# Two edits to the last layer of an attention + gated-MLP kernel: eight pairs at another place modulo 512 bytes, and a group of loaded values in each of two places

## Chip, cores and metric

One core of one Trainium2 chip. The metric is device time in microseconds (us) of one execution, the median of the runs shown. Engines are named as the profile names them: PE is the matrix engine (PEld its weight loads), DVE, ACT and POOL work on vectors, SP issues most of the DMA transfers.

## What is computed

Linear attention with exponential features, and then a gated two-layer MLP on its output, all in float32. Cut to what matters:

```python
# q, k, v: (8, 8, 576, 64); omega: (128, 64)
q_p, k_p = phi(q * scale), phi(k * scale)     # exp(x omega^T - |x|^2/2 - max) / sqrt(m)
num = einsum('bhsm,bhmd->bhsd', q_p, einsum('bhsm,bhsd->bhmd', k_p, v))
den = einsum('bhsm,bhm->bhs', q_p, sum(k_p, axis=2))[..., None] + 1e-06
x = (num / den) as (4608 tokens, 512)
gate = 1 / (1 + exp(-(x @ w_gate)))           # w_gate, w_val: (512, 1536)
out = (gate * (x @ w_val)) @ w_out            # w_out: (1536, 512)
```

## The kernel before

A float32 product is made of three matmuls in the type fp32r: each operand is split into a high part (`yh`, `wh`) and what is left (`yl`, `wl`), and `yl*wh + yh*wl + yh*wh` is summed. The MLP's large products are also cut by a scheme with seven block products instead of eight (`PRODUCT`; the seven operands have index 0 to 6, `N_OPS = 7`).

The program has three stretches. First the attention, which a planner orders with modelled times (`Turns`), mixed with a first part of the MLP (L531: all tokens against the first four of the twelve 128-wide column tiles). Then `second_pass` (L631) makes the other columns, token chunk by token chunk, 128x384 matmuls. The results of both go to DRAM: `ye` holds the values of the first `EP = 2` pairs of column tiles, `yl` (the DRAM tensor) those of the other four pairs, with all seven combinations. Last comes `last(g)` for g = 0 to 17, the last layer: it multiplies the gated values with `w_out`. The change is here.

A group `g` is two times 128 tokens. For each group the loop runs over `j`, the `NPAIR = 6` pairs; below, (g, j) names a pair of a group. For a pair:

- `gated_values` loads its values into a tile `yr` (SP issues it). For j below 2 that is three transfers from `ye`, and `sums` (L741, DVE, four instructions) makes the other combinations. For j of 2 and more it is one transfer of 448 KB from `yl` (L736).
- `parts_of` splits them: ACT copies the values rounded into `yh` (L749), then DVE, or POOL for j = 5 and g above 0, subtracts to get the rest, `yl` (L751). `yh` and `yl` each take one of eight buffers (`buffer`), so four pairs are held at a time, and a buffer comes free when PE has done the pair that lay in it.
- PE does 21 matmuls (L800), 128x128 by 128x256: for each of the seven products the three of the split. The values are the operand that is loaded into the array, the weights `u` are the operand that streams.

After the six pairs, ACT and DVE combine seven sums into the output (`p1`, L816, and seven `add`, L613), and ACT's queue stores it.

The place of a loaded tile before: for g = 0, pairs 0 and 1 lie in the two buffers of tag `xr`, and pairs 2 to 5 in one buffer of tag `u` (as large as one pair of column weights). From g = 1 on, even pairs take turns in the two buffers of `xr`, odd pairs in the two buffers of `ya`, so four pairs are loaded or in use at a time. During group 0 the first three pairs of group 1 are asked for ahead (L808); after that the loads stand in the program at their pair, and the compiler's scheduler sets the engines' order.

The place of `yh` and `yl`: in their buffer, `APART = 16` floats, 64 bytes, from the front. With that the values of a matmul lie 64 bytes behind its streaming weights modulo 512 bytes, in all 2268 matmuls of the last layer. In `second_pass` and in the L531 products both operands of a matmul lie at the same place modulo 512 bytes, which this document calls level.

Of the kernel before, what the change touches and what calls it, by code (L numbers as in the profile page):

```python
# [9 lines left out]
F32 = mybir.dt.float32  # L10
# [10 lines left out]
P = 128  # L21
# [22 lines left out]
NPAIR = NJ // 2  # L44
NE = 4
EP = NE // 2
# [8 lines left out]
UL, UE = 5, 3  # L55


BELOW, APART = 80, 16

FILL = 1e6  # L60
# [26 lines left out]
N_OPS = 7  # L87
# [142 lines left out]
def attn_glu_kernel(ctx: ExitStack, tc, qT, kT, qn, kn, va, om, ident, w, out):  # L230
# [30 lines left out]
    def any_bank(name):  # L261

        n_banks[0] += 1
        return bank(n_banks[0] % 8, name)
# [5 lines left out]
    def pin(ins):  # L270
        return tc.keep_in_program_order(ins) if pinned else ins
# [4 lines left out]
    class Ring(Shelf):  # L276
# [6 lines left out]
        def next(self):  # L283
            return next((p for p in self.places if p[1] == self.at), None)
# [147 lines left out]
    def buffer(name):  # L432
        at, n = (late, XL) if turn_of[0] % (XL + XE) < XL else (tail, XE)
        turn_of[0] += 1
        return at.tile([P, 2, 2, W], F32R, tag="x", bufs=n, name=name)
# [52 lines left out]
    def chunk_loads():  # L488
        for i, (o, n) in enumerate(chunks):
            t = yield from after(arrived[i], 0)  # L490
            t, (r,) = yield from turn("SP", t, xrring)
            raw = load(o, n)
            t = dma(t, 2 * n, KC)
            last = Event(turns, KC)
            for k in range(KC):
                t, (place,) = yield from turn("ACT", t, xring)
                x = keep.tile([P, 2, NC], F32R, tag="x", bufs=XK, name=f"xe{o}_{k}")[:, :, :n]
                nc.scalar.activation(out=x[:, 0], in_=raw[:, k], func=AF.Copy)  # L498
                th = use("ACT", t, act(n), LAG)
                x_of[i, k] = x, place  # L500
                turns.start(chunk_low(i, k, x, raw, n, th, last), -1)
            t = yield from after(last, t)
            xrring.put(r, t)

    def chunk_low(i, k, x, raw, n, t, last):
        t = yield "POOL", t, None, None
        nc.gpsimd.tensor_tensor(out=x[:, 1], in0=raw[:, k], in1=x[:, 0].bitcast(F32), op=ALU.subtract)  # L507
        t = use("POOL", t, pool_(n), LAG)
        x_ready[i][k].set(t)
        last.set(t)  # L510
# [101 lines left out]
    def add(o, a, b):  # L612
        return nc.vector.tensor_tensor(out=o, in0=a, in1=b, op=ALU.add)  # L613
# [70 lines left out]
    def put():  # L684
        while stores:
            to, y = stores.pop(0)
            pin(nc.sync.dma_start(out=to, in_=y))
# [35 lines left out]
        assert not plan  # L723
        return held

    def gated_values(g, j, raw=None):

        if raw is None:
            raw = tail.tile([P, 8, P], F32, tag=("xr", "ya")[j % 2], bufs=2, name=f"yr{g}_{j}")
        t = g // SUB * NW + g % SUB * P  # L730
        if j < EP:
            one, two, both = ye[j, :, 1, t + W : t + W + P], ye[j, :, 0, t + W : t + W + P], ye[j, :, :, t : t + P]
            for to, x in ((raw[:, :2], both), (raw[:, 2], one), (raw[:, 7], two)):
                pin(nc.sync.dma_start(out=to, in_=x))
        else:
            pin(nc.sync.dma_start(out=raw[:, :N_OPS], in_=yl[j - EP, :, g]))  # L736
        return raw

    def sums(raw, pin=lambda x: x):
        for o, a, b, op in ((4, 7, 2, ALU.add), (3, 4, 0, ALU.subtract), (5, 0, 7, ALU.subtract), (6, 1, 3, ALU.subtract)):  # L740
            pin(nc.vector.tensor_tensor(out=raw[:, o], in0=raw[:, a], in1=raw[:, b], op=op))  # L741

    def parts_of(g, j, raw, pin=lambda x: x):
        yh, yl_ = (
            buffer(f"{t}{g}_{j}").rearrange("p a b t -> p (a b t)")[:, APART : APART + N_OPS * P].rearrange("p (o t) -> p o t", t=P)
            for t in ("yh", "yl")
        )
        x = raw[:, :N_OPS]
        pin(nc.scalar.activation(out=yh, in_=x, func=AF.Copy))  # L749
        engine = nc.gpsimd if j == NPAIR - 1 and g else nc.vector  # L750
        pin(engine.tensor_tensor(out=yl_, in0=x, in1=yh.bitcast(F32), op=ALU.subtract))  # L751
        return yh, yl_

    first, ahead = {}, []

    def first_values():

        raws = [gated_values(0, j, tail.tile([P, 8, P], F32, tag="xr", bufs=2, name=f"yr0_{j}")) for j in range(2)]

        def parts(j):  # L760
            first[j] = parts_of(0, j, raws[j], pin)

        def others():
            both = tail.tile([P, NPAIR - 2, N_OPS, P], F32, tag="u", bufs=UE, name="yr0_2")
            raws.extend(gated_values(0, j, both[:, j - 2]) for j in range(2, NPAIR))
            first["raws"] = raws

        c = NCW - 1
        return {
            (c, 2, 2): [lambda: sums(raws[0], pin)],  # L770
            (c, 3, 2): [lambda: sums(raws[1], pin)],
            (c, 7, 0): [lambda: parts(0)],
            (c, 7, 1): [others],
            (c, 7, 2): [lambda: parts(1)],
        }

    def last(g, held=None):

        po = [any_bank(f"po{i}_{g}") for i in range(4)]

        at = {
            n: po[i][:, h * Q : (h + 1) * Q]
            for i, ns in enumerate(((1,), (6, 7), (5, 2), (3, 4))) for h, n in enumerate(ns)
        }
        pin_ = pin if g == 0 else lambda x: x
        for j in range(NPAIR):
            if g == 0 and j in first:
                yh, yl_ = first[j]
            else:
                raw = first["raws"][j] if g == 0 else ahead.pop(0) if ahead else gated_values(g, j)  # L790
                if j < EP:
                    sums(raw)
                yh, yl_ = parts_of(g, j, raw, pin_)
            wh, wl = units[2 * (NPAIR - EP) + j]
            for n, o in at.items():
                i, k = PRODUCT[n]
                i = PLACE[i]
                for m, (u, v) in enumerate(((yl_, wh), (yh, wl), (yh, wh))):
                    pin_(
                        nc.tensor.matmul(  # L800
                            o, lhsT=u[:, i, :], rhs=v[:, k, :],
                            start=(j + m == 0 and n in (1, 6, 5, 3)), stop=(j == NPAIR - 1 and m == 2),
                            skip_group_check=True,
                        )
                    )
            if j == 0 and held is not None:
                next(held, None)
                ahead[:] = [gated_values(1, i) for i in range(3)]  # L808
            elif j == 1 and held is not None:
                put()  # L810
        p1, u2, u3 = (
            late.tile([P, Q], F32, tag=t, bufs=n, name=f"{t}o{g}") for t, n in (("p1", 2), ("u2", 2), ("u3", 1))
        )
        os = tail.tile([P, 2, 2, Q], F32, tag="yb", bufs=1, name=f"o{g}")
        o1, o2 = os[:, 0], os[:, 1]
        nc.scalar.activation(out=p1, in_=at[1], func=AF.Copy)  # L816
        add(u2, at[6], p1)
        add(u3, at[7], u2)
        add(u2, at[5], u2)
        add(o2[:, 1], at[5], u3)  # L820
        add(o1[:, 0], at[2], p1)
        add(o1[:, 1], at[3], u2)
        add(o2[:, 0], at[4], u3)
        t = g // SUB * NW + g % SUB * P
        if g < NCW * SUB - 1:
            for o, r in ((o1, t), (o2, t + W)):
                nc.scalar.dma_start(out=out[r : r + P, :], in_=o)
            return
        for engine, o, i, r in ((nc.sync, o2, 1, t + W), (nc.scalar, o1, 0, t), (nc.scalar, o1, 1, t), (nc.sync, o2, 0, t + W)):
            engine.dma_start(out=out[r : r + P, i * Q : (i + 1) * Q], in_=o[:, i])  # L830
# [298 lines left out]
    with tc.tile_pool(name="early", bufs=1) as early, tc.tile_pool(name="keep", bufs=1) as keep:  # L1129
        with tc.manual_schedule():  # L1130
            with (
# [4 lines left out]
                for key, rank in sorted(order.items(), key=lambda x: x[1]):  # L1136
                    n, *a = key
                    if n[0] == "n":
                        u, b = a
# [53 lines left out]
    tail = ctx.enter_context(tc.tile_pool(name="tail", bufs=1))  # L1193
# [75 lines left out]
```

## Time and profile before

| what | value |
|---|---|
| median of 3 runs | 1081.38 us (1076.92, 1081.38, 1082.26) |
| profiled execution, its own time | 1091.19 us |
| its span, first to last instruction | 1089.4 us |
| PE busy | 1057.5 us, 97% |
| DVE, ACT, POOL busy | 773.0, 490.7, 407.2 us |
| last layer, first to last matmul | about 811.9 to 1084.8 us of the span |

All times of day below are microseconds from the start of the profiled span. The profiled execution is 9.8 us longer than the median of the runs; differences between places of the trace are taken inside the trace. A matmul's shown length (some 280 ns here) is longer than its step to the next one, since matmuls overlap; the pace is read from the starts.

### The profile page before, as it was taken

The numbers are of one execution on the slowest core, as the hardware profiler recorded it, in microseconds if no ns is written. First come the engines' busy times: TensorE is split into PE (matmuls) and PEld (weight loads), VectorE is DVE, ScalarE is ACT, GpSimd is POOL, SyncE is SP. The second block draws the span as 40 slices with busy tenths as digits, with TensorE's granted clock in tenths as the row PEclk, the third lists the DMA queues.
The fourth block names the chain that finished last, engine by engine and source line by source line (L and its number), as shares of the span: only waits on it lengthen the run. The fifth ranks groups of instructions, "written<-read, shape, count | busy, mean of one in ns | idle before, by whom it ended". The sixth has DMA issues, their size and how long they took to land.

```text
span 1089.4 us, 26466 instructions
## 1 busy us (share of the span) xinstructions
PE 1057.5 (97%) x10556; PEld 982.9 (90%) x10556; DVE 773.0 (71%) x1482; ACT 490.7 (45%) x1026; POOL 407.2 (37%) x326
## 2 busy tenths in 40 slices
PE   6789999999999999999999999999999999999998
PEld 5778887878878878899999999999999899999998
DVE  3889998998888856457747574756657777666664
ACT  5777756776456445333323232323223444443442
POOL 0342433342343332126756676756553111111111
PEclk9889999999999999999999999999999999999999
DMA  7587979998768648152424324142897566666663
GB/s 280 179 265 258 323 249 352 306 347 281 264 203 305 226 152 323 48 204 81 146 102 141 121 95 166 52 159 102 295 377 234 185 209 201 191 197 191 197 197 104
DMA packets 121323, 226.32 MB, mean 208 GB/s; under 512 B 10992, under 2 KB 59888, under 8 KB 118128
## 3 DMA queue, kind: packets, MB, share of 16 engines
q1 hardware_dynamic: 115872, 215.39, 58.6%
q10 hardware_dynamic: 5328, 9.24, 2.3%
q8 instruction: 83, 1.36, 0.5%
q14 instruction: 40, 0.33, 0.1%
HBM read 144.90 MB, written 79.69 MB: 206 GB/s over the span
## 4 chain that ended last, share of the span: by engine, by line
PE 87%; DVE 5%; DMA 3%; issue 2%; ACT 2%; POOL 1%; SPq 0%; DVEq 0%; POOLq 0%; ACTq 0%
PE gw L631 32%; PE po L800 23%; PE gv L531 15%; PE pkv L1004 4%; PE ppk L922 3%; PE ppq L922 3%; PE pnq L1069 3%; PE ptq L1052 3%; PE pxq L1094 1%; DMA yr<-yl 1%; ACT kpk L980 1%; DMA xT<-xsq 1%; POOL xe L507 1%; DVE xq L1086 1%; DVE yl L751 1%
## 5 line engine op out<-in xcount | busy, mean ns | idle before, releaser
L631 PE MATMUL gw<-xl,u 128*128 128x384 f32 x2016 | 350.5, 334 | 0.0
L631 PEld LDWEIGHTS gw<-xl,u 128*128 128x128 f32 x2016 | 349.3, 188 | 0.9 <-issue 0.9
L800 PE MATMUL po<-u,yh 128*128 128x256 f32 x1512 | 266.8, 281 | 0.0
L800 PEld LDWEIGHTS po<-u,yh 128*128 128x128 f32 x1512 | 232.9, 190 | 0.0
L800 PE MATMUL po<-u,yl 128*128 128x256 f32 x756 | 212.7, 281 | 3.3 <-DVE yl L751 3.3
L531 PE MATMUL gv<-xe,wh 128*128 128x512 f32 (+1 forms) x640 | 191.1, 378 | 0.9 <-POOL xe L507 0.9
L749 ACT ACTIVATE yh<-yr 128x896 fp32r<-128x896 f32 x108 | 102.2, 952 | 159.0 <-PE po L800 105.8
L800 PEld LDWEIGHTS po<-u,yl 128*128 128x128 f32 x756 | 142.0, 188 | 4.1 <-DVE yl L751 4.1
L531 PEld LDWEIGHTS gv<-xe,wh 128*128 128x128 f32 x640 | 114.4, 189 | 21.3 <-POOL xe L507 1.9
L751 DVE TENSOR_TENSOR yl<-yr,yh 128x896 fp32r<-128x896 f32 x91 | 101.2, 1117 | 40.2 <-ACT yh L749 40.0
L531 PE MATMUL gv<-xe,wl 128*128 128x512 f32 (+1 forms) x320 | 120.9, 378 | 0.2 <-DVE xq L1086 0.2
L751 POOL TENSOR_TENSOR yl<-yr,yh 128x896 fp32r<-128x896 f32 x17 | 36.7, 2161 | 215.7 <-ACT yh L749 203.4
L613 DVE TENSOR_TENSOR u<-gw,p 128x384 f32<-128x384 f32 x96 | 53.3, 555 | 67.0 <-PE gw L631 45.7
L680 POOL TENSOR_TENSOR ya<-ya,g 128x384 f32<-128x384 f32 x48 | 60.0, 1251 | 94.4 <-issue 41.4
L639 ACT ACTIVATE g<-g 128x384 f32<-128x384 f32 x72 | 37.8, 526 | 109.9 <-DVE g L613 109.9
L507 POOL TENSOR_TENSOR xe<-xr,xe 128x512 fp32r<-128x512 f32 (+1 forms) x40 | 51.4, 1308 | 92.0 <-ACT xe L498 91.9
L980 ACT ACTIVATE kpk<-ppk,nbk 128x128 f32<-128x128 f32 x256 | 72.0, 393 | 11.6 <-DVE nbk L938 11.3
L741 DVE TENSOR_TENSOR yr<-yr 128x128 f32<-128x128 f32 x144 | 47.7, 372 | 36.2 <-DMA yr<-ye 34.9
L531 PEld LDWEIGHTS gv<-xe,wl 128*128 128x128 f32 x320 | 60.3, 188 | 10.3 <-issue 0.5
L929 DVE TENSOR_REDUCE sqk<-ppk 128x8 f32<-128x1024 f32 (+1 forms) x48 | 45.2, 953 | 22.1 <-PE ppk L922 22.1
L929 DVE TENSOR_REDUCE sqq<-ppq 128x8 f32<-128x1024 f32 (+1 forms) x48 | 45.5, 955 | 17.3 <-PE ppq L922 16.9
L1057 ACT ACTIVATE qpq<-ptq 128x512 f32<-128x512 f32 (+1 forms) x80 | 41.5, 559 | 36.1 <-PE ptq L1052 35.8
(227 smaller groups left out, 1566.2 us busy)
## 6 DMA issues: line engine op xcount, KB each, us to landing
yr<-yl SPq DMA_DIRECT2D x72, 448.0 KB, 3.9
yl<-ya SPq DMA_DIRECT2D x24, 768.0 KB, 3.5
yl<-yb SPq DMA_DIRECT2D x24, 576.0 KB, 4.5
u<-w_parts SPq DMA_DIRECT2D x6, 1792.0 KB, 10.9
v<-va SPq DMA_DIRECT2D x32, 330.0 KB, 5.4
out<-o ACTq DMA_DIRECT2D x34, 256.0 KB, 2.4
natq<-qn SPq DMA_DIRECT2D x32, 256.0 KB, 5.0
xT<-xsq SPq DMA_DIRECT2D x64, 128.0 KB, 3.0
```

What stands on the lines that cost most here:

```text
L507: nc.gpsimd.tensor_tensor(out=x[:, 1], in0=raw[:, k], in1=x[:, 0].bitcast(F32), op=ALU.subtract)
L531: nc.tensor.matmul(gv, lhsT=u[:, s], rhs=v, start=(m == 0), stop=(m == 3 * KC - 1))
L613: return nc.vector.tensor_tensor(out=o, in0=a, in1=b, op=ALU.add)
L631: nc.tensor.matmul(o, lhsT=u[:, k, s], rhs=v[:, kc, :], start=(first and m == 0), stop=(m == 5), skip_group_check=not first,)
L680: pin(nc.gpsimd.tensor_tensor(out=o, in0=a, in1=b, op=op))
L741: pin(nc.vector.tensor_tensor(out=raw[:, o], in0=raw[:, a], in1=raw[:, b], op=op))
L749: pin(nc.scalar.activation(out=yh, in_=x, func=AF.Copy))
L751: pin(engine.tensor_tensor(out=yl_, in0=x, in1=yh.bitcast(F32), op=ALU.subtract))
L800: nc.tensor.matmul(o, lhsT=u[:, i, :], rhs=v[:, k, :], start=(j + m == 0 and n in (1, 6, 5, 3)), stop=(j == NPAIR - 1 and m == 2), skip_gr ...
L922: nc.tensor.matmul(pp[r, h, k, :], lhsT=raw[HALVES[h], o + r.start : o + r.stop], rhs=om_sb[HALVES[h], :], start=True, stop=True,)
L929: nc.vector.tensor_reduce(out=z[:, :, :, 0], in_=pp, axis=AX.X, op=ALU.max)
L980: nc.scalar.activation(out=kp[t][:, h, :], in_=pp[:, h, i, :], func=AF.Exp, bias=nb[:, h, i : i + 1],)
```

## The change

Two things, both in the last layer.

1. `yh` and `yl` of eight pairs, `LEVELS`, start at the front of their buffer instead of 64 bytes behind it: with that they are level with the weights. They are (0,1), (1,0), (1,4), (2,1), (2,5), (3,3), (6,0) and (12,0), 168 of the 2268 matmuls.
2. Tag `u` gets a second group. Pairs 2 to 5 of group 0 lie in one buffer of it as before; those of group 1 in the next one (the last pair of column weights was there), and from g = 2 on group g reuses the tile of group g - 2. Pairs 0 and 1 of every group have one `xr` buffer each, and `ya` is no longer used for loaded values. All six pairs of group 1 are asked for during group 0, not three.

```diff
+LEVEL = 0
+LEVELS = {(0, 1), (1, 0), (1, 4), (2, 1), (2, 5), (3, 3), (6, 0), (12, 0)}
 BELOW, APART = 80, 16
...
-    def gated_values(g, j, raw=None):
-
-        if raw is None:
-            raw = tail.tile([P, 8, P], F32, tag=("xr", "ya")[j % 2], bufs=2, name=f"yr{g}_{j}")
+    def gated_values(g, j):
+
+        if j < EP:
+            raw = tail.tile([P, 8, P], F32, tag="xr", bufs=2, name=f"yr{g}_{j}")
+        else:
+            if len(groups) == g:
+                groups.append(
+                    tail.tile([P, NPAIR - EP, N_OPS, P], F32, tag="u", bufs=UE, name=f"yr{g}") if g < 2 else groups[g - 2]
+                )
+            raw = groups[g][:, j - EP]
...
     def parts_of(g, j, raw, pin=lambda x: x):
+        at = LEVEL if (g, j) in LEVELS else APART
         yh, yl_ = (
-            buffer(f"{t}{g}_{j}").rearrange("p a b t -> p (a b t)")[:, APART : APART + N_OPS * P].rearrange("p (o t) -> p o t", t=P)
+            buffer(f"{t}{g}_{j}").rearrange("p a b t -> p (a b t)")[:, at : at + N_OPS * P].rearrange("p (o t) -> p o t", t=P)
...
-                ahead[:] = [gated_values(1, i) for i in range(3)]
+                ahead[:] = [gated_values(1, i) for i in range(NPAIR)]
```

The engines' order is the same in both kernels up to group 0 of the last layer. From there it differs on SP and DVE. In the names below the first number after `yr` or `yl` is the pair j, a tile of a whole group has none, and the long number is a running one; `po_0`, `po_1` are the sums of group 0 and 1.

SP from the four loads of group 0 (pairs 2 to 5) on, before:

```order
L736 DMA yr_2_10684<-yl 128x896 x4
L734 DMA yr_0_10754<-ye 128x2x128
L734 DMA yr_0_10754<-ye 128x128 x2
L734 DMA yr_1_10758<-ye 128x2x128
L734 DMA yr_1_10758<-ye 128x128 x2
L736 DMA yr_2_10762<-yl 128x896
L687 DMA yl<-ya_5_10569 128x3x512
L687 DMA yl<-yb_5_10570 128x3x384
L736 DMA yr_3_10988<-yl 128x896
L736 DMA yr_4_11015<-yl 128x896
L736 DMA yr_5_11042<-yl 128x896
L734 DMA yr_0_11087<-ye 128x2x128
```

The same place in the changed kernel:

```order
L745 DMA yr_10684<-yl 128x896 x4
L743 DMA yr_0_10754<-ye 128x2x128
L743 DMA yr_0_10754<-ye 128x128 x2
L743 DMA yr_1_10758<-ye 128x2x128
L743 DMA yr_1_10758<-ye 128x128 x2
L745 DMA yr_10762<-yl 128x896 x4
L690 DMA yl<-ya_5_10569 128x3x512
L690 DMA yl<-yb_5_10570 128x3x384
L743 DMA yr_0_11084<-ye 128x2x128
```

The loads of pairs 3 to 5 of group 1 have moved ahead of the last two stores of `second_pass`, and those of group 2 (`yr_0_11087`, `yr_0_11084`) stand three loads closer behind the stores.

DVE from the output of group 0 to the output of group 1, before (rows of the output's later adds left out at both ends):

```order
L613 TENSOR_TENSOR o_10890<-po_0_10711,u3o_10889 128x256
L751 TENSOR_TENSOR yl_3_10991<-yr_3_10988,yh_3_10990 128x896
L751 TENSOR_TENSOR yl_4_11018<-yr_4_11015,yh_4_11017 128x896
L741 TENSOR_TENSOR yr_0_11087<-yr_0_11087 128x128 x4
L751 TENSOR_TENSOR yl_0_11096<-yr_0_11087,yh_0_11095 128x896
L741 TENSOR_TENSOR yr_1_11120<-yr_1_11120 128x128 x4
L751 TENSOR_TENSOR yl_1_11129<-yr_1_11120,yh_1_11128 128x896
L751 TENSOR_TENSOR yl_2_11156<-yr_2_11153,yh_2_11155 128x896
L613 TENSOR_TENSOR u2o_11070<-po_1_10902,p1o_11069 128x256
```

And in the changed kernel, with the first rows of group 1's output:

```order
L761 TENSOR_TENSOR yl_4_11017<-yr_10762,yh_4_11016 128x896
L616 TENSOR_TENSOR o_10893<-po_0_10710,u3o_10892 128x256
L616 TENSOR_TENSOR o_10893<-po_0_10710,p1o_10890 128x256
L616 TENSOR_TENSOR o_10893<-po_0_10711,u2o_10891 128x256
L616 TENSOR_TENSOR o_10893<-po_0_10711,u3o_10892 128x256
L750 TENSOR_TENSOR yr_0_11084<-yr_0_11084 128x128 x4
L750 TENSOR_TENSOR yr_1_11117<-yr_1_11117 128x128 x4
L761 TENSOR_TENSOR yl_0_11093<-yr_0_11084,yh_0_11092 128x896
L761 TENSOR_TENSOR yl_1_11126<-yr_1_11117,yh_1_11125 128x896
L761 TENSOR_TENSOR yl_2_11152<-yr_10684,yh_2_11151 128x896
L616 TENSOR_TENSOR u2o_11067<-po_1_10905,p1o_11066 128x256
L750 TENSOR_TENSOR yr_0_11272<-yr_0_11272 128x128
```

The subtractions of pairs 3 and 4 of group 1 have moved ahead of the end of group 0's output, and the sums of pairs 0 and 1 of a later group stand earlier: both of group 2 before its first subtraction, and the first of group 3 (`yr_0_11272`) inside group 1's output.

More of the change, by code (lines that the diff above doesn't have):

```diff
@@ L752, in parts_of @@
         return yh, yl_
-    first, ahead = {}, []
+    first, ahead, groups = {}, [], []
     def first_values():
-        raws = [gated_values(0, j, tail.tile([P, 8, P], F32, tag="xr", bufs=2, name=f"yr0_{j}")) for j in range(2)]
+        raws = [gated_values(0, j) for j in range(EP)]
         def parts(j):
@@ L763, in others @@
         def others():
-            both = tail.tile([P, NPAIR - 2, N_OPS, P], F32, tag="u", bufs=UE, name="yr0_2")
-            raws.extend(gated_values(0, j, both[:, j - 2]) for j in range(2, NPAIR))
+            raws.extend(gated_values(0, j) for j in range(EP, NPAIR))
             first["raws"] = raws
```

## Prediction

> **What bounds the kernel now.** I read the page first, then the chain of work that ended last from 780 us on, then the waits of the last layer, then the starts of PE's matmuls one by one.
>
> The page: PE is busy nearly all the time.
>
> ```profile
> PE 1057.5 (97%) x10556; PEld 982.9 (90%) x10556; DVE 773.0 (71%) x1482; ACT 490.7 (45%) x1026; POOL 407.2 (37%) x326
> ```
>
> The chain from 780 us (start, length, what):
>
> ```profile
> 810.01 7.26 DMA yr<-yl
> ...
> 818.34 1.10 DVE yl L751
> ...
> 819.49 9.14 PE po L800 x78
> ...
> 829.92 4.77 DMA yr<-yl
> ...
> 835.77 1.10 DVE yl L751
> ...
> 836.91 10.30 PE po L800 x84
> ...
> 850.66 2.53 DMA yr<-ye
> ...
> 853.29 2.61 DVE yr L741 x3
> ...
> 856.13 1.09 DVE yl L751
> ...
> 857.27 226.41 PE po L800 x1920
> ```
>
> From 857.27 on PE is the whole chain: 1920 matmuls without a wait. Before that the chain leaves PE three times, each time through a load, its splitting on ACT and DVE, and back. What PE itself waited for in the last layer (us in total, times, longest): first from 805 us, then from 820 us, without the first wait.
>
> ```profile
> PE po L800 <- DVE yl L751: 3.3, 4, 2.0
> ```
>
> ```profile
> PE po L800 <- DVE yl L751: 2.9, 3, 2.0
> ```
>
> So waits are 3.3 us of a last layer of 273 us. The rest is the pace, and the pace is not one number. Starts of PE's matmuls at four places; the rows left out between two shown ones of a place are matmuls of the same kind without a gap. First, the fast stretch (42 matmuls from the first row to the last):
>
> ```profile
> 820.97 0.28 PE L800 MATMUL po<-u,yl 128*128 128x256 f32 x1
> ...
> 825.73 0.28 PE L800 MATMUL po<-u,yl 128*128 128x256 f32 x1
> ```
>
> The start of the long stretch (18 matmuls from the second row to the last):
>
> ```profile
> 857.27 0.39 PE L800 MATMUL po<-u,yl 128*128 128x256 f32 x1 [2.04 <-DVE yl L751]
> 857.50 0.40 PE L800 MATMUL po<-u,yh 128*128 128x256 f32 x2
> 857.73 0.28 PE L800 MATMUL po<-u,yl 128*128 128x256 f32 x1
> ...
> 859.85 0.28 PE L800 MATMUL po<-u,yl 128*128 128x256 f32 x1
> ```
>
> An L531 stretch, the same shape with both operands level (15 matmuls):
>
> ```profile
> 112.94 0.28 PE L531 MATMUL gv<-xe,wl 128*128 128x256 f32 x1
> ...
> 114.73 0.28 PE L531 MATMUL gv<-xe,wl 128*128 128x256 f32 x1
> ```
>
> Per three matmuls that is 4.76/14 = 0.340 us in the fast stretch, 2.12/6 = 0.353 in the long one, 1.79/5 = 0.358 for level ones. The first two have the same program, the same places modulo 512 bytes and a full clock:
>
> ```profile
> 821.00:836.00 15.00, 15.00 (x135) 1.00 0.66 225
> ...
> 861.00:876.00 15.00, 15.00 (x130) 1.00 0.68 211
> ...
> 950.00:1000.00 50.00, 50.00 (x426) 1.00 0.65 196
> ```
>
> These rows (stretch, length, PE busy by the last layer's matmuls, their number, clock, DMA share, GB/s) show it again: equal time, equal clock and DMA load, 135 matmuls against 130. So the 64-byte offset has two steady paces. PE takes one of them up after a wait, as the starts show, and keeps it until the next. The fast one holds from pair (0,2) to (1,2), seven pairs; the waits at (1,3), (2,1) and (2,4) end in the slow one, and it lasts to the end. A pair is seven threes: 2.38 us fast, 2.473 slow, 2.51 level.
>
> **The change, part by part.**
>
> *Two places for loaded values.* Why PE waited: with four places a load is asked for when an earlier pair is split, and the queue of SP stands behind that (SPq is SP's queue):
>
> ```profile
> SPq L736 <- DVE yl L751: 52.4, 40, 3.6
> ```
>
> The load at 829.92 of the chain, pair (1,3), begins as a subtraction of group 1 ends; its values are ready at 836.87, when PE already stands. The change asks for it before the last stores, at about 820 to 824: six loads of group 1 and then three more, 0.35 us of issue each as before. Its splitting then waits only for a buffer that PE gave back at 826. Pair (2,1) is late because its load stands in the queue behind those of (1,3) to (1,5); at (2,4) DVE is held by sums, ahead of the subtraction, that wait for the load of 850.66, pair (3,0). Both are now asked for when the same pair of the group before has been split, no longer the pair two later: 4.9 us earlier, more than PE lacked at (2,1) (under 0.9 us: the 2.9 less the 2.0), and about the 2.53 + 2.61 us that stand between the load of (3,0) and PE, of which PE waited 2.0. All three waits should go. A wait costs more than its idle time: the modelled end lies 0.16 us after the next start is due (0.28 - 0.118), and the second matmul starts 0.23 after the first (row of 857.27) where 0.118 is usual. So 2.9 + 3 x (0.16 + 0.11) = **3.7 us**. The first wait stays: the loads of group 0 (810.01, 7.26 us) are unchanged, and their place still waits for PE's last use of column weights.
>
> The stores of `second_pass` that go behind three more loads in SP's queue are read again only by groups 15 to 17, 200 us later: nothing. Their `yb` buffer is also the output's, so group 0's output may start about 1 us later; the sums of group 2 take the other four banks only half a group later: nothing, with half a group, 7 us, as cover. Bytes and numbers of transfers are the same.
>
> *Eight level pairs, by themselves.* The nearest rows are L531's: 2.51 us a pair, 0.04 above slow, 0.13 above fast. Seven replace slow pairs, one, (1,0), a fast one: **+0.4 us**. From below the bound is 0, a pair that keeps the slow pace.
>
> *What they do to the pace behind them.* This is the term that decides, and no row shows a 256-wide level pair followed by an offset pair. A level pair is a disturbance without idle time: its own pace does not depend on what came before, so PE leaves it in the same state each time. Which? Bounds: always slow, 0.65 us of early fast pairs lost (7 x 0.093); always fast, 93 pairs become fast (101 slow ones, less (0,0) and the seven that are level), 93 x 0.0933 = 8.7 us gained. For slow speaks that after the level, 384-wide L631 matmuls the pace was slow at once (15 matmuls from the first row to the last):
>
> ```profile
> 811.55 0.51 PE L631 MATMUL gw<-xl,u 128*128 128x384 f32 x2
> 811.90 0.28 PE L800 MATMUL po<-u,yl 128*128 128x256 f32 x1
> ...
> 813.67 0.28 PE L800 MATMUL po<-u,yl 128*128 128x256 f32 x1
> ```
>
> 1.77/5 = 0.354. But there a matmul lasts longer than the weight load beside it; in a 256-wide one the two are level in length. For fast speaks the start of the fast stretch itself:
>
> ```profile
> 819.71 0.40 PE L800 MATMUL po<-u,yh 128*128 128x256 f32 x2
> 819.95 0.28 PE L800 MATMUL po<-u,yl 128*128 128x256 f32 x1
> 820.06 0.39 PE L800 MATMUL po<-u,yh 128*128 128x256 f32 x2
> ```
>
> Its first two steps are 0.24 us, 0.120 each, the level pace; from there it settles to 0.113. The starts that ended slow had two steps of 0.23 (857.50 to 857.73). PE comes out of a level pair at 0.119 to 0.120 and is nearest to the start that became fast. I take fast, -8.7, and keep both ends.
>
> The Trainium skill, "TensorE: Matmul & The Clock Gate", section "Step-by-step: what each phase is for", says that PE reads the streaming operand and the next weights through two independent ports, so that loading does not slow the running matmul. By that sentence the place modulo 512 bytes is nothing, and the sum would be the 3.7 us alone plus what chance makes of the pace. The trace's two paces at one clock and one shape do not agree with it, but they do not show that the place is their cause.
>
> *Sum.* -3.7 + 0.4 - 8.7 = -12.0 us against the profiled execution, 1091.2 to 1079.2. The median is 9.8 us below that execution; taken off it, 1081.4 - 12.0 = 1069.4, rounded to **1070**.
>
> **The rivals.**
>
> 1. *The runs already have the fast pace.* The profiled execution lies 9.8 us over the median, and all slow pairs made fast are 101 x 0.0933 = 9.4. If the runs without a profile happened to start fast after their waits, only the waits are left to gain: 1081.4 - 3.7 + 0.4 = 1078. For it: those two numbers, and the spread of the three runs, 5.3 us. Against it: of four starts in this trace one became fast, and nothing makes others likelier in a run without a profile.
> 2. *Level pairs leave the slow pace behind.* 1081.4 - 3.7 + 0.4 + 0.65 = 1078.8. For it: the rows at 811.90. From (0,1) on no stretch would be at 0.340.
> 3. *The place does nothing.* Then the eight pairs run as their neighbours, and the one start left, at (0,2), sets the pace to the end: slow 3 times in 4 (1078.4), fast once (99 slow pairs gained, 1081.4 - 3.7 - 9.2 = 1068.5). The sentence of the skill above is this case.
> 4. *Slower: DVE stands still in every group.* The sums of a later group now stand among the output's adds and ahead of subtractions, on a queue that runs in order. Before, DVE already waited for these loads (first row), longest 3.0 us, while ACT was held only by PE's buffers (second row), so it cost nothing:
>
> ```profile
> DVE yr L741 <- DMA yr<-ye: 34.9, 18, 3.0
> ...
> ACT yh L749 <- PE po L800: 105.8, 68, 4.9
> ```
>
> A pair's buffers are free three pairs, 7.4 us, before their next use; ACT's and DVE's parts, 0.95 + 1.12, and the seven adds, 7 x 0.42, leave an estimated 2.4 us, worked out from the rows here and these:
>
> ```profile
> L749 ACT ACTIVATE yh<-yr 128x896 fp32r<-128x896 f32 x108 | 102.2, 952 | 159.0 <-PE po L800 105.8
> L751 DVE TENSOR_TENSOR yl<-yr,yh 128x896 fp32r<-128x896 f32 x91 | 101.2, 1117 | 40.2 <-ACT yh L749 40.0
> L613 DVE TENSOR_TENSOR o<-po,u3o 128x256 f32<-128x256 f32 x36 | 15.0, 416 | 0.0
> ```
>
> It decides from 2.4 us of standing per group on. At the longest wait seen, 3.0, over 16 groups: 16 x (0.6 + 0.27) = 13.9, so 1081.4 - 3.7 + 13.9 = 1092. Against it: each of pairs 0 and 1 has its own place now, so their loads start a group ahead.
>
> **How the numbers follow.** Chances: the forecast 0.50, rival 1 0.15, rival 2 0.18, rival 3 0.09, rival 4 0.08. The forecast's own range is 1066 to 1075: down by the lowest of the three runs (4.5 us under the median, of which I allow three quarters), up where some of the median's pace was fast already. The range to 1080 takes in rivals 1 to 3 and leaves out rival 4. About 0.5%, 5.4 us, is what a measurement of this kernel can tell from no change: faster means under 1076.0. Faster: 0.50 + 0.05 of rival 1 (half fast) + 0.02 of rival 3 = 0.57. Slower: 0.08. Same: 0.35.
>
> **What would show it.** In the changed kernel's trace: PE's waits in the last layer once, at (0,2); SP's waits for DVE's subtractions small; threes at 0.358 in the eight pairs and 0.340 right behind each, to the end, about 2.38 us a pair, the last layer 261 us long. Threes at 0.353 behind (0,1) or (1,0) show rival 2, level pairs at their neighbours' pace rival 3. Waits of PE in groups after 3, with DVE at L750 before them, show rival 4. Wrong in another way it would be if a wait at (1,0), where the values come last, set the pace anew, or if the runs moved by less than their traces.

## The result, and the profile after

The changed kernel is slower: 1087.33 us median of 20 runs (1082.61 to 1089.83) against 1081.59 us of 20 runs of the kernel before (1072.67 to 1092.70), a ratio of 1.005 with a 95% interval of 1.0031 to 1.0069. The forecast was 1070.

Its waits went as forecast. The chain of the profiled execution (1086.45 us, span 1084.6), from 800 us on, leaves PE once for a load and then runs to the end of the last layer:

```profile
808.48 6.37 DMA yr<-yl
...
815.92 1.95 DVE yl L761
...
817.91 261.01 PE po L809 x2214
...
1079.01 0.44 DVE u2o L616
```

Before, two more loads stood in this chain (829.92 and 850.66), and the last uninterrupted stretch began at 857.27. What PE waited for in the last layer (us in total, times, longest):

```profile
PE po L809 <- DVE yl L761: 0.3, 1, 0.3
```

It was 3.3 us in four waits. What did not come is the pace: 261.01 us for 2214 matmuls is 0.1179 us each, the slow one. Four stretches inside the last layer (stretch, length, PE busy, matmuls, clock, DMA share, GB/s): ahead of pair (1,0), inside it, behind it, and between (3,3) and (6,0).

```profile
822.00:826.00 4.00, 4.00 (x38) 1.00 0.93 345
828.00:830.00 2.00, 2.00 (x19) 1.00 0.62 193
831.00:836.00 5.00, 5.00 (x45) 1.00 0.82 256
...
870.00:900.00 30.00, 30.00 (x257) 1.00 0.59 193
```

A stretch also counts the two or three matmuls that reach into it. Ahead of (1,0) there are 38 in 4 us, the fast pace: the one start left, behind the wait at (0,2), was a fast one, as in the trace of before. The starts around the level pair show where that ends:

```profile
827.21 0.28 PE L809 MATMUL po<-u,yl 128*128 128x256 f32 x1
...
827.55 0.28 PE L809 MATMUL po<-u,yl 128*128 128x256 f32 x1
...
827.91 0.28 PE L809 MATMUL po<-u,yl 128*128 128x256 f32 x1
...
829.71 0.28 PE L809 MATMUL po<-u,yl 128*128 128x256 f32 x1
...
830.07 0.28 PE L809 MATMUL po<-u,yl 128*128 128x256 f32 x1
...
830.42 0.28 PE L809 MATMUL po<-u,yl 128*128 128x256 f32 x1
...
830.77 0.28 PE L809 MATMUL po<-u,yl 128*128 128x256 f32 x1
```

Three matmuls take 0.34 us until 827.55, where pair (1,0), the level one, begins; 0.36 inside it, to 830.07; and 0.35 from its successor (1,1) on. No pair comes back to 0.34 until the end. So in this trace the level pair at (1,0) replaced a fast pace by the slow one.

That alone doesn't make it slower than before, whose profiled execution kept the slow pace too. The question was what the other runs of before do.

### The profile page after: what moved, and what is told of

It is laid out like the page before. It is cut to its first block, busy times and chain, and to the rows that moved or that the text cites. A ratio compares the mean times of both kernels' runs of the same rounds, so it can differ in the third digit from the quotient of the medians.

```text
span 1084.6 us, 26358 instructions
## 1 busy us (share of the span) xinstructions
PE 1056.4 (97%) x10556; PEld 982.7 (91%) x10556; DVE 762.2 (70%) x1482; ACT 491.1 (45%) x1026; POOL 406.1 (37%) x326
## 4 chain that ended last, share of the span: by engine, by line
PE 89%; DVE 4%; issue 2%; ACT 2%; DMA 1%; POOL 1%; SPq 0%; DVEq 0%; POOLq 0%; ACTq 0%
PE gw L634 32%; PE po L809 24%; PE gv L534 16%; PE ppq L931 4%; PE pkv L1013 4%; PE ppk L931 3%; PE ptq L1061 3%; PE pnq L1078 3%; PE pxq L1103 1%; ACT kpk L989 1%; POOL xe L510 1%; DMA yr<-yl 1%; DVE hq L1043 1%; DVE xq L1095 0%; DVE sqq L938 0%
## 5 line engine op out<-in xcount | busy, mean ns | idle before, releaser
L809 PEld LDWEIGHTS po<-u,yl 128*128 128x128 f32 x756 | 145.0, 192 | 0.5 <-DVE yl L761 0.5
L931 PE MATMUL ppk<-om_sb,rawk 64*64 64x128 f32 x1152 | 43.7, 292 | 7.9 <-DMA rawk<-kT 4.2
```

The source lines that it names most:

```text
L809: nc.tensor.matmul(o, lhsT=u[:, i, :], rhs=v[:, k, :], start=(j + m == 0 and n in (1, 6, 5, 3)), stop=(j == NPAIR - 1 and m == 2), skip_gr ...
L931: nc.tensor.matmul(pp[r, h, k, :], lhsT=raw[HALVES[h], o + r.start : o + r.stop], rhs=om_sb[HALVES[h], :], start=True, stop=True,)
```

## Experiments

Theory A: a level pair leaves the slow pace behind, and the runs of before keep a fast pace over much of the last layer, which the change takes away. Rival B: the two places, or the order that came with them, cost the time. Rival C, for the last runs: what differs between runs of before lies ahead of the last layer.

The lengths of pairs below are worked out from the starts of the last layer's 2268 matmuls in each trace, 21 to a pair. A start, below, is a place where PE goes on after it stood still.

**The two places alone** (`e1_places`).

```diff
-LEVELS = {(0, 1), (1, 0), (1, 4), (2, 1), (2, 5), (3, 3), (6, 0), (12, 0)}
+LEVELS = set()
```

> The changed kernel with an empty set of level pairs: the two places for loaded values alone. Theory A (a level pair ends the fast pace and leaves the slow one, and the runs of before hold the fast pace for a good part of the last layer): the one start left, behind the wait at (0,2), sets the pace to the end; if it starts fast as in the two traces so far, 0.340 us per three matmuls from (0,2) on, a last layer of about 259 us in the trace, and a median at least 3 us under before (1078 or less). Rival B (the loads in two places, or the order that came with them, cost the time): no better than the changed kernel, 1085 to 1089, with PE waiting or another engine late.

Measured: median 1078.94 us, ratio 0.999 (0.9954 to 1.0025). The runs fall apart: six from 1072.84 to 1078.00, one at 1079.87, five from 1086.24 to 1087.62. The traced one was of the upper group, 1087.02 us: its one start, at (0,2), was slow, and it kept the pace to the end:

```profile
PE po L809 <- DVE yl L761: 0.3, 1, 0.3
```

```profile
822.00:850.00 28.00, 28.00 (x240) 1.00 0.82 267
950.00:1000.00 50.00, 50.00 (x427) 1.00 0.61 203
```

So without waits behind it, the first start sets the pace of the 105 pairs from (0,3) on, worth 105 x 0.0933 = 9.8 us. The groups lie 13 us apart; no run of the lower one was traced, so its fast start is an inference, and the other 3 us lie elsewhere: the five lowest runs have a mean granted clock of 0.993 or 0.994, the five highest 0.988 to 0.992, and the last experiment shows what that does ahead of the last layer. Against B: the changed kernel without its level pairs had runs up to 14 us under the changed kernel's median. The median, 2.5 us under before's 1081.42, is not clear of noise, and the traced start was not the fast one that the expectation took from two traces.

**The eight level pairs alone** (`e2_levels`): before, with the line `at = LEVEL if (g, j) in LEVELS else APART` in `parts_of` and nothing else.

> The kernel before with the eight level pairs alone; its loads and order are unchanged. Theory A: slow pace behind each level pair, 0.353 us per three; the waits at (1,3), (2,1) and (2,4) stay and may start a fast stretch, but the next level pair ends it at the latest; about 3.7 us of waits more than the changed kernel, 1086 to 1092. Rival B: about the time of before, 1080 to 1083.

Measured: 1089.51 us (1085.98 to 1090.91), ratio 1.0074 (1.0050 to 1.0099). Fast ahead of (1,0), slow from there on:

```profile
820.00:825.00 5.00, 5.00 (x47) 1.00 0.76 277
...
829.00:833.00 4.00, 4.00 (x37) 1.00 1.00 339
950.00:1000.00 50.00, 50.00 (x427) 1.00 0.64 191
```

The level pairs by themselves make the kernel slower. A predicted that, B did not. That the two places win some of it back is not shown, since the interval overlaps that of the changed kernel. The trace, of the lowest of the eight runs, waited 2.1 us in two places. The wait at (2,4) ended in a fast start (2.502 us for that pair, as at (0,2); a slow start takes 2.58), and the level pair (2,5) behind it brought the slow pace back.

**Which offsets are fast** (`e3_scan`, `e4_scan_back`, `e6_fine_up`, `e7_fine_down`): the two places, no level pairs, another offset in each group.

```diff
-        at = LEVEL if (g, j) in LEVELS else APART
+        at = (8 * g if g < 16 else 4 * (g - 15)) % P      # e3_scan
+        at = 8 * (17 - g) % P if g > 1 else APART         # e4_scan_back
+        at = 6 + g                                        # e6_fine_up
+        at = 23 - g                                       # e7_fine_down
```

> Two places, no level pairs, and another offset in every group: groups 0 to 15 start their values 8 x g floats behind the buffer's front (0, 8, 16, ... 120), groups 16 and 17 by 4 and 8. Only the pace per group is of interest. If the place modulo 512 bytes sets the pace, groups differ: 2.51 to 2.52 us a pair at offset 0, 2.38 or 2.473 at 16, others unknown between 2.24 (256 columns at full clock, 107 ns) and 2.52. If the place does nothing, all groups behind the one wait run at one pace.

> The same with the offsets in falling order: 16 in groups 0 and 1, then 120, 112, ... 16, 8, 0 in groups 2 to 17. An offset with one steady pace shows the pace of the rising order; one that keeps the pace it is entered with may show the other. For 16 the entry is then from 24, not from 8: theory A's two paces would allow a change there, a single pace per offset would not.

> Two places, no level pairs, offset 6 + g floats in group g, so 6 to 23 in rising order. Theory A: about 2.485 us a pair near 8, 2.38 at 16 since it is entered from 15; where the fast pace begins and ends, and whether any offset is faster than 2.38, is open. If only the last entry and not the offset counted, all would stay at the first pace.

> The same in falling order, 23 to 6. Theory A: 2.473 at 16, entered from above, and the two orders agree where an offset has a single pace. An offset that is fast in both orders would need no set of other pairs.

14 us inside groups of the rising scan: offset 8, 16, 24 and 80, which is 16 plus 256 bytes.

```profile
826.50:840.50 14.00, 14.00 (x121) 1.00 0.75 229
841.50:855.50 14.00, 14.00 (x126) 1.00 0.68 213
856.00:870.00 14.00, 14.00 (x119) 1.00 0.58 198
960.50:974.50 14.00, 14.00 (x126) 1.00 0.61 202
```

And of the falling one, 24 and then 16:

```profile
1022.50:1036.50 14.00, 14.00 (x121) 1.00 0.57 199
1037.20:1051.20 14.00, 14.00 (x121) 1.00 0.55 199
```

16 is fast behind 8 and slow behind 24, at the same place, without a wait between. The length of a settled pair (the mean of a group's third to fifth, good to 0.002), in us:

| offset (floats) | rising | falling |
|---|---|---|
| 0 and 64 | 2.520 | 2.520 |
| 8, 72 | 2.485 | 2.485 |
| 16, 80 | 2.380 | 2.473 |
| 24, 88 | 2.520 | 2.463 |
| 32, 96 | 2.491 | 2.491 |
| 40, 104 | 2.520 | 2.520 |
| 48, 112 | 2.473 | 2.473 |
| 56, 120 | 2.473 | 2.450 |
| 6 | 2.491 | 2.560 |
| 12 | 2.473 | 2.473 |
| 13 | 2.380 | 2.380 |
| 14 | 2.474 | 2.473 |
| 15 | 2.51 | 2.51 |
| 16 (from 15, from 17) | 2.380 | 2.380 |
| 19 | 2.520 | 2.380 |
| 21 | 2.520 | 2.520 |
| 22 | 2.380 | 2.380 |

(The value at 6 in the rising order is that of its last two pairs, as a wait lies ahead of the third. The offsets left out, 7, 9 to 11, 17, 18, 20 and 23, agree in both orders, between 2.450 and 2.520.)

Three things follow. The pace depends on the place; it repeats every 64 floats, 256 bytes; and some offsets (6, 16, 19, 24 and 56) have two paces, and which one comes depends on how they are entered. It is not the side alone: 16 entered from above was 2.473 behind 24, but 2.380 behind 17, where 2.473 was expected. Offset 0, level, is always 2.520 (2.517 for a single pair), and what came behind a level pair at 16 was slow in seven cases of seven in the changed kernel and in `e2_levels` each; the eighth, (0,1), is followed by a wait. Eleven of these fourteen level pairs were entered at the slow pace and three at the fast one ((1,0) in both traces, (2,5) in `e2_levels`); all were left at the slow one. The scans moved the loaded operand only, so they don't tell its place against the streaming one from its place in memory as such.

**Level pairs at 8 floats** (`e5_level8`): one number of the changed kernel.

```diff
-LEVEL = 0
+LEVEL = 8
```

> The changed kernel with one number changed: the eight pairs start 8 floats (32 bytes) behind the buffer's front, not 0. Theory A, as the scans have refined it (the pace at offset 16 is the one that it is entered with: fast behind offset 8, slow behind 24 and behind 0): a pair at 8 takes about 2.485 us, every pair behind one 2.38, so the last layer takes about 261 us in the trace at the latest from (1,1) on, and every run is a fast one, 1071 to 1077, with the fast group of the places-only kernel (1073 to 1075) plus 0.8 us as the likeliest. Rival B (two places or their order cost time): 1082 to 1088, as the changed kernel.

Measured: 1083.36 us, ratio 1.001 (0.9982 to 1.0037), between the two cases. A group at 8 led to fast in the scans, but one pair of it does so only now and then. Slow behind (3,3); fast behind (6,0), for six groups; slow behind (12,0):

```profile
874.00:900.00 26.00, 26.00 (x223) 1.00 0.59 199
930.00:980.00 50.00, 50.00 (x443) 1.00 0.67 221
1000.00:1050.00 50.00, 50.00 (x427) 1.00 0.60 198
```

In its trace two of the pairs at 8 that were entered slow ((2,1), (6,0)) were left fast, and all three that were entered fast ((1,0), (2,5), (12,0)) were left slow. So a set of pairs that locks the fast pace was not found; the expectation failed here.

**Other offsets for all pairs** (`e10_apart13`, `e11_apart22`), and 13 and 22 entered from many places (`e12_entry`). The two places, `LEVELS = set()` and

```diff
-BELOW, APART = 80, 16
+BELOW, APART = 80, 13      # e10_apart13; 22 in e11_apart22
```

```diff
+        at = {0: 4 * g, 1: 13, 2: 13, 3: 4 * g, 4: 22, 5: 22}[j] % P      # e12_entry
```

> Two places, no level pairs, all values 13 floats (52 bytes) behind the weights instead of 16. The scans were fast at 13 from both sides. If 13 has the fast pace alone, every run is fast: 1071 to 1076, with the last layer at about 260 us. If it too has two paces, the runs fall in two groups some 13 us apart, as those at 16 did (1073 to 1075 and 1086 to 1088).

> The same at 22 floats (88 bytes), also fast from both sides in the scans. The same two outcomes; in the scan it took less to settle than 13 did (2.385 to 2.390 us in its first pair against 2.397 to 2.405), so if one of the two is fast alone, 22 is the likelier.

> Two places; in each group pair 0 and pair 3 start 4 x g floats behind the front (0 to 68), pairs 1 and 2 13 floats, pairs 4 and 5 22 floats. So 13 and 22 are entered from 18 places. An offset with one pace shows 2.38 us in its second pair after every entry; one with two shows 2.47 or so after some, and says after which.

Measured: 1077.20 us, ratio 0.9944 (0.9910 to 0.9978), at 13, and 1076.89 us, 0.9945 (0.9911 to 0.9979), at 22. Both are faster than the kernel before, and their medians, taken at another time, lie 10 us under the changed kernel's. From the two places at 16 floats (0.999, 0.9954 to 1.0025) they are not told apart: the intervals overlap. In each trace all 105 pairs from (0,3) on run at 2.380; this row is of the one at 22:

```profile
950.00:1000.00 50.00, 50.00 (x443) 1.00 0.64 207
```

The runs reach from 1071.4 to 1079.7 with one at 1087.3 (13), and from 1072.3 to 1084.3 (22). They don't fall into two groups as at 16, but the highest were not traced, and `e12_entry` shows that 13 and 22 do have other paces: of 17 entries without a wait 13 settled at 2.38 to 2.39 in 15 and stayed at 2.52 in two (behind 20 and 36); of 18 entries 22 settled at 2.38 to 2.39 in 15 and stayed at 2.45 in three (behind 0, 44 and 64). The level offsets, 0 and 64, are two of those three. In the same trace 48, which took 2.473 in both scans, ran at 2.380 behind 13 and behind 22.

**The second pass** (`e8_pass2`, `e16_pass2_96`): a pad in each of two pools moves the eight `x` buffers 64 (96) bytes down, with the last layer's offsets raised by as much. The run at 64 bytes is otherwise `e5_level8`, the run at 96 bytes `e11_apart22`.

```diff
+        if c == 1:
+            tail.tile([P, 112], F32, tag="pad", bufs=1, name="pad_tail")      # 104 for 96 bytes
...
+                late.tile([P, 16], F32, tag="pad", bufs=1, name="pad_late")   # 24
```

> The kernel with pairs at offset 8, and two pads (64 bytes, 448 bytes) that move the eight value buffers 64 bytes down, so that in the second pass too the loaded operand lies 64 bytes behind the streaming one modulo 256 bytes; the last layer's two offsets are 64 bytes larger for it, at the same places relative to the weights. If the place modulo 256 bytes costs the 384-wide level matmuls what it costs 256-wide ones (0.120 against 0.113 us), their step goes from 0.173 to about 0.167 us, 2016 x 0.0067 = 13 us, and the median to about 1060; with a slow pace of its own, 1065 to 1072. If only matmuls whose length equals their weight load feel the place, the step stays at 0.173 and the time is that of the kernel with pairs at 8.

> All last-layer values 22 floats (88 bytes) behind the weights, as in the kernel that was 0.55% faster, and the second pass's loaded operand 96 bytes behind its streaming one (two pads, 96 and 416 bytes). At 64 bytes its step rose from 0.1734 to 0.1767 us. If the 384-wide matmuls have a fast pace at some offset as the 256-wide ones do, 96 is as good a trial as any: 0.167 us would give 13 us, 1064. If their length beyond the weight load makes level the best place, 0.174 to 0.177 and 1077 to 1084.

Measured: 1088.81 us, ratio 1.0057 (1.0027 to 1.0086), at 64 bytes, and 1079.41, 0.9952 (0.9923 to 0.9981), at 96. 50 us of the second pass, at 64, at 96, and level in the kernel before:

```profile
500.00:550.00 50.00, 50.00 (x285) 1.00 0.35 125
```

```profile
500.00:550.00 50.00, 50.00 (x290) 1.00 0.36 130
```

```profile
500.00:550.00 50.00, 50.00 (x289) 1.00 0.39 141
```

The step, from all starts that lie less than 0.2 us apart, is 176.7 ns at 64 bytes against 173.4 at 96 and level. 96 bytes gained nothing on top of the 22 floats (0.9945). 64 bytes lost 5.4 us between the medians of `e5_level8` and `e8_pass2`; the longer steps of 2016 matmuls alone, 3.3 ns each, make an estimated 6.7 us. The 1060 to 1072 of the first expectation did not come; a fast pace for the 384-wide matmuls was not found at these two places.

**The kernel before, four more traces** (`e9_before_again`, `e13_before_2`, `e14_before_3`, `e15_before_4`), unchanged.

> The kernel before once more, unchanged, for a second trace of it; the first one, at 1091.2 us, was slow from (1,3) on. Theory A (slower because the runs of before hold the fast pace for a good part): at a time near the median of 1081 to 1082 this trace shows some 60 to 100 pairs at 2.38 us, at one near 1077 nearly all, at one near 1090 few; each 10 fast pairs take 0.93 us off. Rival C (the first trace was slow for something outside the last layer, such as the clock's start): the same pace at a shorter time, and the difference lies ahead of 800 us.

> The kernel before, a third trace. Theory A: its time follows the number of fast pairs in its last layer and its waits, once the start of the last layer is taken off: time = start of the last layer + 273.0 us, less 0.093 us for each fast pair above 7 and less the waits below 3.7 us, + 6.5 us of tail and launch. At 1077 to 1082 that needs 40 to 100 fast pairs, a run like the fast group of the places-only kernel. Rival C: few fast pairs at such a time; then the runs of before are shorter ahead of the last layer, which would start at 800 us or earlier.

> The kernel before, a fourth trace, with the same two readings: many fast pairs at a time near 1080 (theory A), or few and an early start of the last layer (rival C).

> The kernel before, a fifth trace, with the same two readings: many fast pairs at a time near 1080 (theory A), or few and an early start of the last layer (rival C).

| trace | time, us | last layer begins | its length | pairs at 2.38 |
|---|---|---|---|---|
| the profile before | 1091.19 | 811.9 | 272.9 | 5 |
| e9 | 1084.93 | 809.7 | 268.9 | 11 |
| e13 | 1084.43 | 812.0 | 266.0 | 97 |
| e14 | 1078.57 | 810.6 | 261.5 | 103 |
| e15 | 1077.32 | 806.5 | 264.4 | 101 |
| changed | 1086.45 | 810.4 | 269.7 | 3 |

(Pairs that a wait or the settling behind it falls into don't count as fast here, so the profile before has 5 where the prediction spoke of a stretch of seven.) The last stretches of the chain in these four, in the order of the table; the shown wait before each differs, but 1794 and 1920 matmuls can be compared:

```profile
865.87 211.57 PE po L800 x1794
```

```profile
857.38 219.52 PE po L800 x1920
```

```profile
867.45 203.63 PE po L800 x1794
```

```profile
850.48 219.35 PE po L800 x1920
```

The first is slow (0.1179 us each), the others fast (0.1143, 0.1135, 0.1142); the prediction's row had 226.41 us for 1920. Three of five traces of before are fast from their last wait on, in spite of up to 3.8 us of waits. In all five, ten of 15 starts became fast (two of the 15 lie behind a gap of only 0.2 us).

The second and the fourth row hold something that no wait shows: behind the wait at (2,4), of 2.0 us in e13 and 2.3 us in e15, the granted clock was 0.50 for some 3 us, and a matmul's step 0.213 us. That took another 1.6 and 1.4 us. The profile before waited 2.0 us at the same pair and kept its clock.

Rival C holds for a part: the last layer's start moves too, by 5.5 us, but not with the pace. It moves with the granted clock of the first 80 us: that was 0.91 in e15, in the trace of `e2_levels` and in that of `e11_apart22`, whose last layers begin at 806.5, 808.0 and 807.2; it was 0.87 to 0.89 in the other four traces of before, 809.7 to 812.0. So pace, waits and start must be read together: e13 has 97 fast pairs and took only 0.5 us less than e9 with 11, since it began 2.3 us later and waited longer.

## Why the prediction was wrong, point by point

*The waits.* Right in kind: three of four went, and the last layer of the changed kernel is 3.2 us shorter than in the profile before (269.7 against 272.9). As a gain against the median it stood on one trace: the five traces of before waited 3.3, 0.5, 3.8, 1.7 and 2.9 us, and in two of them the half clock behind the wait at (2,4) came on top. The price of a wait in the prediction has no such term.

*The level pairs by themselves.* Right: 2.517 us a pair, 0.044 above slow six times and 0.14 above fast once; the eighth, (0,1), lies beside a wait.

*The pace behind them.* This step failed. The prediction took fast, -8.7 us, because the one start that became fast began with steps of 0.12 us, the level pace. Behind the fourteen level pairs at 0 that no wait follows the pace was slow. The sign itself doesn't hold: in `e1_places` the start at (0,2) began with two steps of 0.24 us together (818.70 to 818.94) and became slow, and in e13 and e14 starts that began with 0.23 became fast. The row that it had set aside, slow behind the level L631 matmuls at 811.90, was the better guide: behind 256-wide level matmuls it is the same. Against the profile before, rival 2's terms give -3.7 + 0.4 + 0.65 = -2.65 us; the last layers differ by -3.2.

*The base.* Also failed: the sum took the profiled execution's pace as typical and its 9.8 us over the median as something that the change leaves alone. The other four traces of before lie at a mean of 1081.3 us, 9.9 below it, and 7.7 of these are their shorter last layers (265.2 against 272.9): it was a run with few fast pairs. That one start in four becomes fast was a small sample; it is ten in 15. Rival 1 (the runs have the fast pace already) was true in three traces of five and rival 2 (level leaves the slow one) throughout, and the prediction priced each alone, at 1078 and 1078.8, both under before. Together they give what was seen: the change removes waits, and takes away a fast pace that is worth more. In numbers of the traces: the changed kernel's, 1086.45 us, is 3.2 us longer than the mean of the five of before, 1083.3, and 3.0 of these lie in the last layer (269.7 against a mean of 266.7). The medians of the runs differ by 5.7; where the other 2.6 lie is not shown, and the start of the last layer alone moves by 5.5 us between traces.

*Rival 3.* The Trainium skill ("TensorE: Matmul & The Clock Gate", "Step-by-step: what each phase is for") says that PE reads the streaming operand and the next weights through two independent ports, so that loading takes no read bandwidth from the running matmul. The prediction drew from it that the place may be nothing. The runs disagree with that: the same matmuls at the same clock take 2.38 to 2.56 us a pair, and two offsets with one pace in all scans, 7 and 0, differ by their place alone, at 2.450 and 2.520. The measurement decides.

*Rival 4.* It did not come: PE didn't wait after group 0. The prediction's sign, that SP's waits for DVE's subtractions would be small, failed without a cost: SP waited 139.4 us for them, as a load is now asked for long ahead.

```profile
SPq L743 <- DVE yl L761: 139.4, 31, 9.0
```

## What to carry to other kernels

When one kernel's runs spread by more than a per cent, read the pace of its matmuls in several traces before you price a change against one: a steady state that an accident at its start selects can be worth more than all visible waits. Removing waits removes the occasions at which that state is chosen anew, which fits the two places alone with their runs from 1073 to 1080 and near 1087 us. An offset that is fast from most entries (13 or 22 floats here) did more than eight pairs meant to reset the pace, and it is found with another offset in each group of one traced kernel.

## What the runs showed of the hardware

- A 256-wide fp32r matmul behind a weight load of its own ran at seven or more steady steps, 113.3 to 121.9 ns, as the place of the loaded operand was moved, with a period of 256 bytes.
- At several offsets two steps are steady. At 16 floats the one that a start took stayed for over 1900 matmuls.
- 384-wide ones were 173.4 ns at 0 and 96 bytes, 176.7 at 64.
- Behind a wait of PE of 2.0 and 2.3 us the granted clock was 0.50 for some 3 us in two traces, and stayed 1.00 behind one of 2.0 us in a third.
- Why the place matters was not shown.
